# Spreading the second layer around the turn between two networks, and a new order for the last three pairs

## The chip, the cores and the metric

The kernel runs on one core of a Trainium2 chip. The metric is device time in microseconds (us) of one execution. Five engines matter: TensorE (PE, matrix products), VectorE (DVE), ScalarE (ACT), GpSimd (POOL), and the DMA queue that SyncE (SP) issues. PE writes to PSUM, eight banks of 512 single-precision columns by 128 partitions; VectorE and ScalarE read them and write there too, GpSimd does not.

## The reference

```python
# attention with a decay per head (4 batches, 8 heads, 576 positions, 64 wide), no softmax
ret = scale * (q @ k^T) * Dmat          # Dmat[i, j] = gamma_h ** (i - j) for i >= j, else 0
x = (ret @ v)                           # turned to 2304 tokens x 512
# mixture: 8 experts, 512 -> 1024 -> 512
P = exp(x @ w_gate - max); 8 rounds of normalising rows and columns of P
x = sum over e of P[:, e] * (relu(x @ w1[e]) @ w2[e])
# second network: 512 -> 2048 -> 512
h = x @ w_in
out = max(0.01 * h, h) @ w_out
```

## The kernel before, in words

After the attention, both networks run as one list of **units**. A unit is 512 hidden columns: the 8 experts give units 0 to 15 (`NU1` = 16, two per expert, `UPE`), the second network gives units 16 to 19. The 2304 tokens are held as two halves of 1152; one **step** takes a unit and a third of the tokens (`s` = 0, 1, 2; three tiles `jj` of 128 tokens from each half). So there are 60 steps, numbered 0 to 59 here: steps 42 to 44 are unit 14, steps 45 to 47 unit 15 (the last of the mixture), step 48 is the first of the second network. `edge` is 48, `NS` is 3.

Every product of two matrices is done with seven block products in place of eight (a Strassen form), and every operand is split into a high and a low half-precision part, so that one block product is several matmuls.

**First layer** (`product_h`, line 960): per step two groups `g` of 7 products, 14 in all (`PH`), each of six matmuls 384 wide, into the banks `hA`, `hB`, `hD`, `hE`. ScalarE and VectorE take them out, and `splits` (line 1021) makes from them the hidden tiles `hp` and `hs` (high part on ScalarE, low part on VectorE), the stationary operands of the second layer.

**Second layer** (`group_s`, line 1108): per step three **pairs** (one per `jj`; `pairs` counts them over all steps, 180), per pair five groups numbered `what` = 0 to 4, seven products of six matmuls 256 wide. A pair has two banks, `t1` (from `s1`, the tiles `s1a` and `s1b`) and `t2` (from `s2`, shown as `s`); pairs take the two bank pairs in turn (`at % 2`). Group 0: products 1 and 5 into the left and right half of `t1`; ScalarE copies the left half to the right half of `t2` (`seed`), and VectorE later adds the right half of `t1` to the result `yb` (`gather`, put off through the queue "evac" and issued at the latest before group 2). Group 1: product 6 onto the right half of `t2`, gathered to `ya`. Group 2: products 2 and 3 onto `t1`, gathered to `ya` 512 wide. Group 3: product 7 onto the right half of `t2`, copied to its left half. Group 4: product 4 onto the left half, and both halves gathered to `yb`. In units 0 and 15 (`PLAIN`) the second layer is done plainly, in four groups of six matmuls 512 wide (lines 1171 to 1190) and an empty group 4, from the hidden blocks as they are.

**The order.** All instructions are issued by one program in the order of the list `groups` (line 1332): group 0 of a pair stands before group 4 of the pair before it, so the list runs one group ahead; the last pairs of unit 15's steps are kept whole. `seconds_by(h)` (line 1349) tells how many groups are to be issued after `h` first-layer products: step `n`'s 15 groups (`GS`) begin at `14 (n + 1) + 6` (`LAG` = 6) and spread over `span` products. At the end of the program the rest of the list, the last 22 groups, runs with no first-layer products between. The other work (evacuations, weight preparation, the turn) stands in queues of `Order` (line 64), which books estimated times for each engine and issues a task when its inputs and its engine should be free; tasks that a product needs are forced out before it (`flush`, `need`). A queue looks at its first 12 tasks, the turn's at 48.

**The turn** (`turn_steps`, line 1247, and `operand_tasks`, line 467): when a pair of unit 15 is complete, its two result tiles are normed (sums on ScalarE or VectorE, factors on VectorE), scaled on GpSimd (line 1274), transposed on PE through an idle second-layer bank (line 1284), copied out, combined on GpSimd (lines 484 to 491), split on ScalarE and VectorE, stored to memory and loaded again as x of the second network. Steps 48, 49 and 50 need the x that steps 45, 46 and 47 end.

**Weights**: `prep_steps` (line 178) prepares unit `u + 1` while unit `u` runs: a load, eight magnitude sums (line 191), a maximum through PE, scaling on ScalarE, splits and differences on ScalarE and GpSimd. A second-layer weight buffer is free when the step two units back has ended.

Of the kernel before, what the change touches and what calls it, by code (L numbers as in the profile page):

```python
# [23 lines left out]
UPE = F // FU  # L24
# [7 lines left out]
NS = HT // ST  # L32
# [10 lines left out]
COST = {"A": (0.2, 0.00089), "D": (0.17, 0.00105), "G": (0.28, 0.0020)}  # L43
LAT, SLACK, WINDOW = 0.15, 0.6, (12, 48)
LAG = 6
PLAIN = (0, NU1 - 1)
XST, R64 = 4, 2

# [75 lines left out]
def retention_moe_ffn_kernel(ctx: ExitStack, tc: tile.TileContext, qk, vk, wg, wm, wf,  # L124
# [43 lines left out]
    order = Order()  # L168
# [9 lines left out]
    def prep_steps(u, small_bank):  # L178
# [105 lines left out]
        def add(eng, n, f, deps=(), key=None, cond=None, lat=LAT):  # L284
            x = Task(eng, n, f, deps, (u,) + key, cond, lat)
            tasks.append(x)
            return x
# [32 lines left out]
        def split(part, g, pre, key, cond=None):  # L320
            pre = tuple(pre)
            if part and u in PLAIN:
                hb = [add("A", 512, high_p(g, h), pre, key, cond) for h in range(2)]
# [206 lines left out]
    def bank_a(name):  # L530

        return ps.tile([P, 512], F32, tag="a", name=name, bufs=5)

    def bank_b(name):

        return ps.tile([P, 512], F32, tag="l1", name=name, bufs=1)
# [331 lines left out]
    hA, hB, hD, hE, s1a = (bank_a(n) for n in ("hA", "hB", "hD", "hE", "s1a"))  # L868
    s1 = [s1a, bank_b("s1b")]
    s2 = [ps.tile([P, 512], F32, tag=f"du{i}", name=f"s2_{i}", bufs=1) for i in range(2)]  # L870
# [72 lines left out]
    def work(tag, n=1, bufs=1):  # L943
        return gpool.tile([P, n, ST], F32, tag=tag, name=f"{tag}_{len(h_done)}", bufs=bufs)

    evac, until, h_last = {}, {}, {}
# [13 lines left out]
    def product_h(u, s, g, r):  # L960
# [50 lines left out]
        else:  # L1011
            order.flush("hid", lambda k: k[:3] != (u, s, g))
            tmp["fs"] = work("fs", 4)
            bent(tmp["fs"][:, 2] if u in PLAIN or u >= NU1 else D_, D_, u, HS)
            evac[4] = act()
# [5 lines left out]
    def splits(u, s, g, what):  # L1021
# [52 lines left out]
        else:  # L1074
            a11, a12, a22 = (fp[:, i] for i in range(3))
            d = evac[4]
            a21 = hD[:, :ST] if moe else fs[:, 2]
            if u in PLAIN:
                one = fs[:, 2:3]
# [28 lines left out]
    def group_s(u, s, jj, what):  # L1108

        j = NT_S * s + jj  # L1110
        ya, yb = y[j], y[NJ + j]
        if what == 0 and jj == 0:
            need_hid(u, s)
            if s == 0:
                need((u, "w2"))
            if u == UPE:
                order.flush("gate", lambda k: True)
            factors(u, s)
        fa, fb = fac[u][:, j:j + 1], fac[u][:, NJ + j:NJ + j + 1]
        at = pairs.index((u, s, jj))  # L1120
        t1, t2 = s1[at % 2], s2[at % 2]
        order.wait(until.get(("s", what < 2 if u in PLAIN else what in (0, 2), at % 2)))
        if what == 0:
            last_pair[0] = at
            if jj == 0:
                order.wait(h_last[u, s].done)
        left, right = slice(0, DH), slice(DH, DM)
        first = u == 0 or u == NU1
        ts = slice(128 * jj, 128 * jj + 128)

        def product(r, out_, start):
            xi, wi = PROD[r]
            k = 0
            for g in range(2):
                t, i = (hid[u, s, g, "p"], xi) if xi < 3 else (hid[u, s, g, "s"], xi - 3)
                w = wtiles[u, 1, g]
                for a, b in ((0, 0), (0, 1), (1, 0)):
                    nc.tensor.matmul(out_, t[:, a, i, ts], w[:, b, wi, 0, :], start=start and k == 0, stop=k == 5,  # L1138
                                     skip_group_check=True)
                    k += 1  # L1140
            order.t += 6 * (DH / 2400 + 0.004)

        def gather(out_, bank, f, new):
            n = bank.shape[-1]
            b = ("s", what < 2 if u in PLAIN else what in (0, 2), at % 2)
            ev = max(order.t + 0.2, until.get(b, 0.0) + LAT)
            if new:
                nc.scalar.activation(out_, bank, AF.Copy, scale=f)
                until[b] = order.book("A", n, ev)
            else:  # L1150
                nc.vector.scalar_tensor_tensor(out_, bank, f, out_, op0=ALU.mult, op1=ALU.add)  # L1151
                until[b] = order.book("D", n, ev)

        def seed(out_, bank):
            b = ("s", False, at % 2)
            nc.scalar.copy(out_, bank)  # L1156
            until[b] = order.book("A", DH, max(order.t + 0.2, until.get(b, 0.0) + LAT))
            if what == 0:
                until["s", True, at % 2] = until[b]

        def close():
            if jj == NT_S - 1:
                s_done.add((u, s))
            if u == NU1 - 1:
                turn_steps(s, j)

        if what == 0:
            if u == UPE:
                for i in (j, NJ + j):
                    nc.vector.tensor_scalar(y[i], y[i], prob[:, i, 0:1], None, op0=ALU.mult)  # L1170
        if u in PLAIN:
            if what == 4:
                return
            h, l = divmod(what, 2)
            bank = (t1, t2)[h].rearrange("p (a n) -> p a n", a=2)
            for g in range(2):
                part, i = (("p", l), ("p" if l else "s", 2 * l))[h]
                w, t = wtiles[u, 1, g][:, :, slice(1, 3) if l else slice(0, 4, 3), 0], hid[u, s, g, part]
                for q, (a, b) in enumerate(((0, 0), (0, 1), (1, 0))):
                    nc.tensor.matmul(bank, t[:, a, i, ts], w[:, b], start=l == g == q == 0, stop=l == g == 1 and q == 2,  # L1180
                                     skip_group_check=True)
                order.t += 3 * (DM / 2400 + 0.004)
                if g == 0:
                    tick(0)
            if l:
                gather((ya, yb)[h], (t1, t2)[h], (fa, fb)[h], first)
                if h:
                    close()
            tick(0)
            return  # L1190
        if what == 0:
            product(1, t1[:, left], True)
            tick(0)
            product(5, t1[:, right], False)
            seed(t2[:, right], t1[:, left])
            b = ("s", True, at % 2)
            sd = Task(None, 0, None, done=until[b])

            def f():
                gather(yb[:, right], t1[:, right], fb, first)  # L1200
            order.queues["evac"].append(Task("A" if first else "D", 0, f, (sd,), ("s", at)))
            tick(0)
        elif what == 1:
            product(6, t2[:, right], False)
            gather(ya[:, right], t2[:, right], fa, first)
            tick(0)
        elif what == 2:
            order.flush("evac", lambda k: k == ("s", at))
            order.wait(until.get(("s", True, at % 2)))
            product(2, t1[:, left], False)  # L1210
            tick(0)
            product(3, t1[:, right], False)
            if first:
                gather(ya[:, left], t1[:, left], fa, True)
                gather(ya[:, right], t1[:, right], fa, False)
            else:
                gather(ya, t1, fa, False)
            tick(0)
            if u == NU - 1:
                put(0, j)  # L1220
        elif what == 3:
            product(7, t2[:, right], False)
            seed(t2[:, left], t2[:, right])
            tick(0)
        else:
            product(4, t2[:, left], False)
            if first:
                gather(yb[:, left], t2[:, left], fb, True)
                gather(yb[:, right], t2[:, right], fb, False)
            else:  # L1230
                gather(yb, t2, fb, False)
            tick(0)
            if u == NU - 1:
                put(1, j)
            close()
# [69 lines left out]
    def tick(n):  # L1305

        order.t += n * (1 / 2400) + (0.009 if n else 0)
        wait[0] -= 1
        if drain and wait[0] <= 0:
            wait[0], f = drain.pop(0)  # L1310
            f()
        order.pump()
        try_loads()
# [17 lines left out]
    pairs = [(u, s, jj) for u, s in stages for jj in range(NT_S)]  # L1331
    groups = []
    whole = lambda p: p[0] == NU1 - 1 and p[2] == NT_S - 1
    for i, p in enumerate(pairs):
# [4 lines left out]
        if whole(p):  # L1339
            groups.append((*p, 4))  # L1340
    groups.append((*pairs[-1], 4))
    GS, PH = 5 * NT_S, 2 * len(H_ORDER)
    edge = stages.index((NU1, 0))
    spos, hpos = [0], [0]
# [4 lines left out]
    def seconds_by(h):  # L1349

        for n in range(len(stages) - 1, -1, -1):
            a = PH * (n + 1) + max(LAG, 13 - 3 * n)
            if h >= a:
                span = PH if n < edge - UPE * NS or n >= edge else PH - LAG
                return GS * n + min(GS, (h - a) * GS // span)
        return 0

# [101 lines left out]
```

## Time and profile before

| | |
|---|---|
| median of 3 runs | 1855.32 us (1853.75 to 1855.46) |
| profiled execution | 1855.54 us, span 1853.8 us, granted clock 0.988 |
| PE busy | 1795.8 us, 97% of the span, 13800 matmuls |
| VectorE, ScalarE, GpSimd busy | 1487.6 us (80%), 1261.7 us (68%), 823.9 us (44%) |
| chain that ended last | PE 87%, VectorE 6%, GpSimd 3%, ScalarE 1% |
| DMA | 276.67 MB, 48% of the 16 engines' time in the slices' mean |

How to read it: busy time of PE is the union of its matmuls, whose ends are modelled, so the distance between the starts of two products says more than the busy share. In the page's picture of 40 slices PE stands at 9 tenths almost everywhere; below it lie the first two slices, two from 1483 to 1576 us, where the second network begins, and the last. In a row of the timeline the bracket gives how long the engine was idle before, and which engine and line released it.

### The profile page before, as it was taken

Reading aid. Unit: us, or ns where it says so; the run is one execution under the profiler, and the core shown is the slowest. Engines: PE = TensorE matmul, PEld = TensorE weight load, DVE = VectorE, ACT = ScalarE, POOL = GpSimd, SP = SyncE. Lnnn points to the kernel's source line nnn. Section 1 sums busy time; section 2 is a strip of 40 time slices with the busy share of each in tenths; the row PEclk is TensorE's granted clock in tenths of the full one; section 3 lists DMA queues with packets and bytes.
Section 4 is the critical chain, followed back from the end, with each engine's and each line's share of the span. In section 5 each row is a group of like instructions: output and inputs, shape, how many; then the busy total and the mean of one; then the engine's idle time right before and its main releaser. Section 6 shows DMA issues by size and latency. Waiting matters only on the chain.

```text
span 1853.8 us, 35942 instructions
## 1 busy us (share of the span) xinstructions
PE 1795.8 (97%) x13800; PEld 1303.5 (70%) x13800; DVE 1487.6 (80%) x2576; ACT 1261.7 (68%) x2659; POOL 823.9 (44%) x786
## 2 busy tenths in 40 slices
PE   8899999999999999999999999999999987999997
PEld 7755577777777777777777777777675555777776
DVE  6755888998888888888888888888766885688875
ACT  5567677767676677767676777767565675876753
POOL 4633353626354453625254453726225961443600
PEclk9899999999999999999999999999999998999999
DMA  9874455355354454454354454455243454335242
GB/s 339 294 229 143 131 151 158 121 158 170 109 180 121 152 158 142 129 165 151 116 181 130 141 160 142 124 170 159 89 140 111 154 160 125 122 106 156 84 122 75
DMA packets 207857, 276.67 MB, mean 149 GB/s; under 512 B 13874, under 2 KB 177860, under 8 KB 202564
## 3 DMA queue, kind: packets, MB, share of 16 engines
q1 hardware_dynamic: 207684, 274.37, 47.4%
q8 instruction: 108, 1.77, 0.4%
q14 instruction: 65, 0.53, 0.1%
HBM read 244.69 MB, written 29.63 MB: 148 GB/s over the span
## 4 chain that ended last, share of the span: by engine, by line
PE 87%; DVE 6%; POOL 3%; ACT 1%; issue 1%; DMA 1%; SPq 0%; DVEq 0%; ACTq 0%; POOLq 0%
PE s L1138 16%; PE hB L968 12%; PE hA L968 12%; PE hE L968 12%; PE s1a L1138 11%; PE s1b L1138 11%; PE hD L968 6%; PE s L1180 2%; DVE y L1151 1%; PE s1a L1180 1%; PE sc L639 1%; PE s1b L1180 1%; PE xo L666 1%; DMA x<-x 1%; DVE xst L513 1%
## 5 line engine op out<-in xcount | busy, mean ns | idle before, releaser
L968 PEld LDWEIGHTS <-w 128*128 128x128 f16 x5040 | 492.0, 98 | 274.0 <-issue 14.0
L1138 PEld LDWEIGHTS <-hs 128*128 128x128 f16 x3888 | 380.3, 98 | 89.1 <-DVE hs L1059 5.8
L1138 PEld LDWEIGHTS <-hp 128*128 128x128 f16 x2916 | 285.7, 98 | 89.5 <-issue 12.9
L254 POOL TENSOR_TENSOR w<-raw,w 128x384 f16<-128x384 f32 x152 | 164.1, 1095 | 393.9 <-ACT w L244 393.8
L1151 DVE SCALAR_TENSOR_TENSOR y<-s,fac,y 128x256 f32<-128x256 f32 (+1 forms) x324 | 198.4, 614 | 114.7 <-PE s L1138 94.8
L261 POOL TENSOR_TENSOR raw<-raw 128x256 f32<-128x256 f32 x304 | 281.3, 925 | 20.0
L968 PE MATMUL hE<-x,w 128*128 128x384 f16 x1440 | 276.6, 327 | 6.1 <-DMA x<-x 2.9
L968 PE MATMUL hB<-x,w 128*128 128x384 f16 x1440 | 277.3, 328 | 4.4 <-ACT hB L978 4.3
L968 PE MATMUL hA<-x,w 128*128 128x384 f16 x1440 | 276.8, 328 | 4.2 <-ACT w L244 2.3
L1138 PE MATMUL s<-w,hs 128*128 128x256 f16 x1944 | 265.9, 273 | 1.6 <-ACT s L1156 1.5
L1059 DVE TENSOR_TENSOR hs<-fs,hs 128x768 f16<-128x768 f32 (+1 forms) x228 | 241.6, 1062 | 8.0 <-ACT hs L1049 7.1
L279 POOL TENSOR_TENSOR w<-raw,w 128x512 f16<-128x512 f32 x148 | 200.4, 1369 | 72.3 <-ACT w L273 71.8
L1049 ACT ACTIVATE hs<-fs 128x768 f16<-128x768 f32 (+1 forms) x228 | 187.6, 824 | 41.7 <-DVE fs L1084 32.0
L408 POOL TENSOR_TENSOR f<-f,e 128x256 f32<-128x256 f32 x64 | 54.9, 858 | 355.6 <-DVE e L400 355.6
L1049 ACT ACTIVATE hp<-fp 128x384 f16<-128x384 f32 x240 | 160.2, 677 | 11.8 <-DVE fp L1007 11.0
L1151 DVE SCALAR_TENSOR_TENSOR y<-s1a,fac,y 128x256 f32<-128x256 f32 (+1 forms) x161 | 98.6, 613 | 54.8 <-ACT s L1156 26.5
L1151 DVE SCALAR_TENSOR_TENSOR y<-s1b,fac,y 128x512 f32<-128x512 f32 (+1 forms) x163 | 99.9, 613 | 49.2 <-PE s1b L1138 22.6
L1138 PE MATMUL s1b<-w,hs 128*128 128x256 f16 x972 | 134.1, 274 | 5.1 <-DVE hs L1059 2.8
L1138 PE MATMUL s1a<-w,hp 128*128 128x256 f16 x972 | 133.2, 273 | 5.8 <-DVE mr L207 3.5
L968 PE MATMUL hD<-x,w 128*128 128x384 f16 x720 | 137.0, 326 | 0.0
L1138 PE MATMUL s1a<-w,hs 128*128 128x256 f16 x972 | 133.9, 273 | 2.8 <-ACT hs L1049 1.5
L1138 PE MATMUL s1b<-w,hp 128*128 128x256 f16 x972 | 133.3, 273 | 2.8 <-DVE y L1151 2.3
(199 smaller groups left out, 2694.7 us busy)
## 6 DMA issues: line engine op xcount, KB each, us to landing
x<-x SPq DMA_DIRECT2D x420, 384.0 KB, 4.1
raw<-in_wm SPq DMA_DIRECT2D x32, 1024.0 KB, 8.1
r<-in_wf SPq DMA_DIRECT2D x64, 256.0 KB, 2.7
qk<-in_qk SPq DMA_DIRECT2D x16, 512.0 KB, 5.8
vk<-in_vk SPq DMA_DIRECT2D x16, 512.0 KB, 5.8
wf_s<-f SPq DMA_DIRECT2D x32, 256.0 KB, 2.7
raw<-wf_s SPq DMA_DIRECT2D x8, 1024.0 KB
x<-xst SPq DMA_DIRECT2D x30, 256.0 KB, 2.8
```

Of the source, the lines that this page charges most:

```text
L254: nc.gpsimd.tensor_tensor(v[0], v[1], v[2], op=ALU.subtract)
L261: nc.gpsimd.tensor_tensor(o, x, y_, op=ALU.subtract)
L279: (nc.gpsimd if u or part else nc.vector).tensor_tensor(lo, r, hi, op=ALU.subtract)
L408: nc.gpsimd.tensor_tensor(dst, dst, cur["tx"].bitcast(F32), op=ALU.mult)
L513: nc.vector.tensor_tensor(st[d][:, :, 1], src[d](), st[d][:, :, 0], op=ALU.subtract)
L639: nc.tensor.matmul(scv[j][:w, m, :w], kv[r, m, :], qv[r, m, :], start=True, stop=True)
L968: nc.tensor.matmul(bank, w[:, a, wi, k, :], x[:, :, b, k, :], start=r in (1, 5) and k == q == 0, stop=k == 1 and q == 2, skip_group_check= ...
L1049: nc.scalar.activation(hid[k][:, 0, a:b], src[:, a:b], AF.Relu if moe and relu else AF.Copy)
L1059: nc.vector.tensor_tensor(t[:, 1, a:b], src[:, a:b], t[:, 0, a:b], op=ALU.subtract)
L1138: nc.tensor.matmul(out_, t[:, a, i, ts], w[:, b, wi, 0, :], start=start and k == 0, stop=k == 5, skip_group_check=True)
L1151: nc.vector.scalar_tensor_tensor(out_, bank, f, out_, op0=ALU.mult, op1=ALU.add)
L1180: nc.tensor.matmul(bank, t[:, a, i, ts], w[:, b], start=l == g == q == 0, stop=l == g == 1 and q == 2, skip_group_check=True)
```

## The change

Three things change. The squeeze of the second layer (`span`, line 1354) covered steps 42 to 47 with 8 products; now it covers steps 45 to 47 with 10, and steps 42 to 44 spread over 14 like all others. In step 59 the last pair (`at` = 179) takes `hA` and `hB` as its two banks, through the index `bi`, which also replaces `at % 2` in the keys of the booked times; its group 3 gathers the right half of `t2` at once, and its group 4 only the left half. And the last sixteen entries of `groups` are written out by hand: with A, B, C for the last three pairs and Z for the one before them, the order was A0 Z4 A1 A2 A3 B0 A4 B1 B2 B3 C0 B4 C1 C2 C3 C4 and is now A0 Z4 A1 B0 A2 B1 C0 A3 B2 C1 A4 B3 C2 C3 B4 C4. No product is added or removed; one gather is cut in two.

```diff
--- before.py
+++ after.py
@@ -43,6 +43,7 @@
 COST = {"A": (0.2, 0.00089), "D": (0.17, 0.00105), "G": (0.28, 0.0020)}
 LAT, SLACK, WINDOW = 0.15, 0.6, (12, 48)
 LAG = 6
+EARLY = 4
 PLAIN = (0, NU1 - 1)
 XST, R64 = 4, 2
 
@@ -1118,8 +1119,9 @@
             factors(u, s)
         fa, fb = fac[u][:, j:j + 1], fac[u][:, NJ + j:NJ + j + 1]
         at = pairs.index((u, s, jj))
-        t1, t2 = s1[at % 2], s2[at % 2]
-        order.wait(until.get(("s", what < 2 if u in PLAIN else what in (0, 2), at % 2)))
+        bi = 2 if at == len(pairs) - 1 else at % 2
+        t1, t2 = (*s1, hA)[bi], (*s2, hB)[bi]
+        order.wait(until.get(("s", what < 2 if u in PLAIN else what in (0, 2), bi)))
         if what == 0:
             last_pair[0] = at
             if jj == 0:
@@ -1142,7 +1144,7 @@
 
         def gather(out_, bank, f, new):
             n = bank.shape[-1]
-            b = ("s", what < 2 if u in PLAIN else what in (0, 2), at % 2)
+            b = ("s", what < 2 if u in PLAIN else what in (0, 2), bi)
             ev = max(order.t + 0.2, until.get(b, 0.0) + LAT)
             if new:
                 nc.scalar.activation(out_, bank, AF.Copy, scale=f)
@@ -1152,11 +1154,11 @@
                 until[b] = order.book("D", n, ev)
 
         def seed(out_, bank):
-            b = ("s", False, at % 2)
+            b = ("s", False, bi)
             nc.scalar.copy(out_, bank)
             until[b] = order.book("A", DH, max(order.t + 0.2, until.get(b, 0.0) + LAT))
             if what == 0:
-                until["s", True, at % 2] = until[b]
+                until["s", True, bi] = until[b]
 
         def close():
             if jj == NT_S - 1:
@@ -1193,7 +1195,7 @@
             tick(0)
             product(5, t1[:, right], False)
             seed(t2[:, right], t1[:, left])
-            b = ("s", True, at % 2)
+            b = ("s", True, bi)
             sd = Task(None, 0, None, done=until[b])
 
             def f():
@@ -1206,7 +1208,7 @@
             tick(0)
         elif what == 2:
             order.flush("evac", lambda k: k == ("s", at))
-            order.wait(until.get(("s", True, at % 2)))
+            order.wait(until.get(("s", True, bi)))
             product(2, t1[:, left], False)
             tick(0)
             product(3, t1[:, right], False)
@@ -1221,12 +1223,15 @@
         elif what == 3:
             product(7, t2[:, right], False)
             seed(t2[:, left], t2[:, right])
+            if bi == 2:
+                gather(yb[:, right], t2[:, right], fb, False)
             tick(0)
         else:
             product(4, t2[:, left], False)
-            if first:
-                gather(yb[:, left], t2[:, left], fb, True)
-                gather(yb[:, right], t2[:, right], fb, False)
+            if first or bi == 2:
+                gather(yb[:, left], t2[:, left], fb, first)
+                if first:
+                    gather(yb[:, right], t2[:, right], fb, False)
             else:
                 gather(yb, t2, fb, False)
             tick(0)
@@ -1339,6 +1344,9 @@
         if whole(p):
             groups.append((*p, 4))
     groups.append((*pairs[-1], 4))
+    end = [(p, w) for p, w in zip((0, -1, 0, 1, 0, 1, 2, 0, 1, 2, 0, 1, 2, 2, 1, 2),
+                                  (0, 4, 1, 0, 2, 1, 0, 3, 2, 1, 4, 3, 2, 3, 4, 4))]
+    groups[-16:] = [(*pairs[p - 3], w) for p, w in end]
     GS, PH = 5 * NT_S, 2 * len(H_ORDER)
     edge = stages.index((NU1, 0))
     spos, hpos = [0], [0]
@@ -1351,7 +1359,7 @@
         for n in range(len(stages) - 1, -1, -1):
             a = PH * (n + 1) + max(LAG, 13 - 3 * n)
             if h >= a:
-                span = PH if n < edge - UPE * NS or n >= edge else PH - LAG
+                span = PH - EARLY * (edge - NS <= n < edge)
                 return GS * n + min(GS, (h - a) * GS // span)
         return 0
 
```

## Rows read from the trace of the kernel before

**Rows 1.** Windows: stretch; its length; busy time (instructions) by engine; granted clock; DMA share; GB/s

```profile
160.00:1300.00 1140.00, 1136.09 (x8532) 832.36 (x8530) 980.69 (x1720) 813.47 (x1702) 530.68 (x509) 1.00 0.48 147
1330.00:1340.00 10.00, 7.51 (x48) 4.72 (x46) 7.44 (x11) 5.21 (x9) 2.98 (x2) 0.86 0.28 79
```

**Rows 2.** Timeline of PE, end of step 43: start, length, instructions, idle before

```profile
1333.68 0.49 PE L1138 MATMUL s1b<-w,hs 128*128 128x256 f16 x3
1336.06 0.39 PE L1138 MATMUL s1b<-w,hs 128*128 128x256 f16 x2 [1.89 <-ACT hs L1049]
...
1337.17 2.08 PE L968 MATMUL hA<-x,w 128*128 128x384 f16 x6
1339.05 1.91 PE L968 MATMUL hE<-x,w 128*128 128x384 f16 x6
1340.80 1.14 PE L968 MATMUL hB<-x,w 128*128 128x384 f16 x6
```

**Rows 3.** Timeline of PE, end of step 44

```profile
1365.60 0.49 PE L1138 MATMUL s1a<-w,hs 128*128 128x256 f16 x3
1367.30 0.39 PE L1138 MATMUL s1a<-w,hs 128*128 128x256 f16 x2 [1.21 <-ACT hs L1049]
1368.29 0.28 PE L1138 MATMUL s1a<-w,hs 128*128 128x256 f16 x1 [0.60 <-DVE hs L1059]
```

**Rows 4.** Timeline of PE, start of step 50

```profile
1524.41 0.82 PE L1138 MATMUL s1b<-w,hs 128*128 128x256 f16 x6
1526.71 1.14 PE L968 MATMUL hA<-x,w 128*128 128x384 f16 x6 [1.48 <-DMA x<-x]
1527.68 0.82 PE L1138 MATMUL s<-w,hs 128*128 128x256 f16 x6
1531.41 1.79 PE L968 MATMUL hE<-x,w 128*128 128x384 f16 x6 [2.91 <-DMA x<-x]
...
1535.38 1.14 PE L968 MATMUL hB<-x,w 128*128 128x384 f16 x6
```

**Rows 5.** Timeline of PE, start of step 51

```profile
1561.88 0.82 PE L1138 MATMUL s1a<-w,hs 128*128 128x256 f16 x6
1564.98 0.50 PE L968 MATMUL hA<-x,w 128*128 128x384 f16 x2 [2.28 <-ACT w L244]
...
1575.89 1.27 PE L968 MATMUL hB<-x,w 128*128 128x384 f16 x6
```

**Rows 6.** Timeline of ScalarE: magnitude sums of unit 17's weights

```profile
1523.36 0.62 ACT L191 ACTIVATE junk<-raw 128x512 bf16<-128x512 f32 x1
...
1545.35 0.61 ACT L191 ACTIVATE junk<-raw 128x512 bf16<-128x512 f32 x1
```

**Rows 7.** Line 1274 on GpSimd: least, median, longest in ns; first and last start

```profile
L1274 POOL TENSOR_SCALAR y<-y,ts x18: 1559/1644/2779, 1412.7 to 1506.8; 128x512 f32<-128x512 f32 x18
```

**Rows 8.** Timeline of PE, the last pair

```profile
1843.67 0.82 PE L1138 MATMUL s<-w,hs 128*128 128x256 f16 x6
1845.51 0.81 PE L1138 MATMUL s1b<-w,hp 128*128 128x256 f16 x6 [1.02 <-DVE y L1151]
...
1846.82 0.82 PE L1138 MATMUL s<-w,hs 128*128 128x256 f16 x6
1848.08 0.81 PE L1138 MATMUL s<-w,hp 128*128 128x256 f16 x6 [0.44 <-ACT s L1156]
```

**Rows 9.** Timeline of VectorE, the last pair's gathers

```profile
1843.93 1.14 DVE L1151 SCALAR_TENSOR_TENSOR y<-s,fac,y 128x512 f32<-128x512 f32 x2 [1.92 <-PE s L1138]
1844.98 0.48 DVE L1151 SCALAR_TENSOR_TENSOR y<-s1b,fac,y 128x256 f32<-128x256 f32 x1
...
1848.99 0.75 DVE L1151 SCALAR_TENSOR_TENSOR y<-s,fac,y 128x512 f32<-128x512 f32 x1 [1.22 <-PE s L1138]
```

**Rows 10.** Timeline of VectorE, reading a bank behind ScalarE

```profile
1359.11 0.56 DVE L1002 SCALAR_TENSOR_TENSOR fp<-hB,p 128x384 f32<-128x384 f32 x1 [0.51 <-ACT hD L996]
```

**Rows 11.** DMA issues of the last stores: count, KB each, median us to landing

```profile
out<-y SPq DMA_DIRECT2D x4, 128.0 KB, 2.4
```

## The prediction

> **What bounds the kernel now.** I read the windows first, to see where TensorE (PE) is not full. From 160 to 1300 us it is busy 1136.09 of 1140 us at full clock [rows 1]: there nothing but its own work counts. A change of order can only win in the rest, so I followed PE's timeline there. What it loses is the excess of start-to-start distances over the undisturbed ones, 0.97 us for a first-layer product (six matmuls) and 0.66 us for a second-layer one, both read off where such rows come. Five places matter.
>
> At the end of step 43 the first group of the next step is issued right behind the last first-layer product, and its last three matmuls wait for hidden tiles that ScalarE and VectorE are still splitting. Three matmuls take 0.33 us, so 1333.68 to 1336.06 loses 2.05 us and 1336.06 to 1337.17 another 0.78. The next two first-layer products then run 1.88 and 1.75 us apart in place of 0.97 (0.9 and 0.8 lost) [rows 2]: the granted clock, 1.0 elsewhere, is 0.86 in the mean of 1330 to 1340 [rows 1], so for a while it stood at the lower level, 1.2 GHz, after those waits. Together 4.5 us.
>
> One step later the same happens: 1.70 - 0.33 = 1.37 and 0.99 - 0.22 = 0.77 us [rows 3], 2.1 us. Here the short waits are followed by no slow products.
>
> At the start of step 50 PE waits for the turned x. From 1524.41 to 1526.71 it loses 2.30 - 0.66 = 1.6; 1526.71 to 1527.68 is an undisturbed first-layer product; from 1527.68 to 1531.41 it loses 3.1; and the three products to 1535.38 take 3.97 in place of 0.97 + 2 x 0.66, 1.7 more [rows 4].
>
> At the start of step 51 the weights of unit 17 are late. From 1561.88 to 1575.89 four second-layer and two first-layer products run, 4 x 0.66 + 2 x 0.97 = 4.6 us of work in 14.0: 9.4 us lost [rows 5].
>
> In the last sixteen groups PE stops three times between a pair's groups 1 and 2 (1843.67 to 1845.51 is 1.84 - 0.66 = 1.18; the other two are 1.13 and 1.19) and once before the last group (1.26 - 0.66 = 0.60); 1845.51 to 1846.82 shows two undisturbed products. Together 4.1 us [rows 8].
>
> **First part: steps 42 to 44 are no longer squeezed.** A step's 15 groups go between first-layer products, from the 6th product of the next step on. Before, steps 42 to 47 did it within 8 products, so they ended exactly with that next step, and where units run in plain order of the list the last of the 15 is already the first group of the step after it. Its hidden tiles come from the product just issued: this is what rows 2 and 3 show. Spread over 14 products this group comes six products later, as in the steps of [rows 1], which lose next to nothing. The split chain takes 3.5 us (1333.68 to 1337.17), six products alone 5.8, so it is covered. No instruction is added or removed; 7 of the 15 groups move past first-layer products. Gain 4.5 + 2.1 = 6.6 us. Bounds: 4.9 if the clock loss of 1.7 comes elsewhere instead, and 6.6, all that the rows hold; I take 6.6, by the like steps of rows 1. At the boundary after step 44 PE doesn't wait now, so nothing is won there. What could be late next is whatever needs the end of these steps: the second-layer weight buffers of unit 16 wait for step 44, now 6 products later. But the weight queue looks only 12 tasks ahead, and the twelve before them wait for the first half of step 47 in any case, which hides it; uncovered it is those six products, 5.8 us, off a preparation that has the whole of step 48 left.
>
> **Second part: steps 45 to 47 spread over 10 products, not 8.** Their y is turned (scaled, transposed, summed, split, stored, loaded) into the x of steps 48 to 50. A step's three tiles are complete 1, 1 and 2 first-layer products later than before. PE waits for a load of x only at step 50 [rows 4], so steps 48 and 49 have cover. At step 50 the last tile's transposes wait for the buffers of the tile before it; it is that tile's delay, one product, that passes on: +1.0 us. Bounds: 0 (the looser spread lets VectorE and ScalarE, which serve turn and groups together, be faster by as much) and 1.95 (two products). Shorter waits for scaled y inside steps 48 and 49 I leave as they are. Behind step 50 all moves along, unit 17's weights included, so the 9.4 us stay; the rivals hold their bounds.
>
> **Third part: the last three pairs over three bank pairs.** The products stay 22. A pair's group 2 overwrites its first bank, so it waits for the gather of that bank's right half, which stands on VectorE behind two others (start to start 1.05 us for these two, then 0.48 for itself [rows 9]). In the new order two groups or more lie between a pair's 1 and 2. I followed all sixteen with 0.66 us per product, 0.66 and 0.39 from a wide and a narrow gather to the next, and 0.44 from a product past ScalarE's copy to the next product (end of 1846.82's to 1848.08 [rows 8]): each of the three gathers ends 0.2 to 2.8 us before its bank is wanted, in whichever of the two places VectorE's order gives it. So 1.13, 1.18 and 1.19 go, and the 0.60 too, since that copy now lies beside the second pair's last group. New is a wait: the last pair's right half is gathered behind that copy, on the same bank. Two engines that only read one bank are ordered in this kernel: VectorE stood 0.51 us for ScalarE's copy out of hB before it read hB itself [rows 10]. So the gather ends 0.49 us after PE could have begun the last group; only the final gather is queued behind it. That is 256 wide instead of 512, 0.75 - 0.48 = 0.27 less [rows 9]. Sum 4.1 - 0.49 + 0.27 = 3.9 us. Of the banks taken, hA and hB, the last first-layer readers are done before these groups begin. Issue, landing and end of the last stores I take as they are, 2.4 us to landing [rows 11]. Bounds: 1.5 (the last three gathers end within 2.2 us of each other, so gathers queue and stores crowd) and 4.4 (no order between readers).
> The Trainium skill, "DMA: Bandwidth & Descriptors", section "Latency and other measured facts", puts most of a transfer's fixed cost on the receipt from HBM, 0.2 us on average and 2 us at high load. By that rule the crowded last stores could land up to 1.8 us later, an estimate from that page, and this part would be worth 2.1. The trace has no crowded stores that bear it out.
>
> **Sum.** -6.6 + 1.0 - 3.9 = -9.5 us on the profiled execution of 1855.54 us (span 1853.8). The median of the runs is 0.2 lower than it. Forecast **1846.0**, with 1842 to 1850 as its own range.
>
> **Rivals.**
> *The turn slows (1854).* POOL scales 18 tiles in 1.56 to 2.78 us each, median 1.64 [rows 7]; the six of the last step stand in the chain to step 50's x. If the new spread puts VectorE's splits beside them so that all take the longest, that is 6 x 1.14 = 6.8 us, and 0.95 for the second product: 1846.0 + 7.8 = 1853.8. For it: both engines are crowded there. Against: the same work stands in nearly the same order, and the longest is rare. The Trainium skill, "SBUF — State Buffer", section "Who interferes with whom", has the mechanism: a VectorE operation with two SBUF inputs and a reading GpSimd instruction exclude each other. By that rule the spread from 1.56 to 2.78 is what one would see; no row names the partner.
>
> *Unit 17's weights fall behind (1863, slower).* The last of the eight magnitude sums comes at 1545.35, 22 us after the one before [rows 6], because ScalarE is booked for other work; what follows it is forced at the start of step 51. If the later turn pushes that sum to the forced point, 1562.5, the chain behind it moves by 17.2 us: 1846.0 + 17.2 = 1863. It beats the whole gain from a slip of 9.5 us on. For it: the choice goes by booked times and has jumped 22 us already. Against: the turn moves by a product or two.
>
> *They come in time (1837).* If that sum goes out beside its neighbours, up to 9.4 us of step 51 go: 1846.0 - 9.4 = 1836.6. For and against as above, mirrored.
>
> *The third part doesn't do what it says* (a gather elsewhere in VectorE's order than I followed): 3.9 less, 1849.9, inside the forecast's own range.
>
> **Chances.** Forecast 0.50, slow turn 0.18, late weights 0.14, early weights 0.18. About 0.2%, 3.7 us, is what a measurement of this kernel can tell from no change. The slow turn (1850 to 1855) splits half between faster and same, and a few per cent of forecast and late weights are same. Faster 0.76, same 0.10, slower 0.14. The range goes from 1838.5 (the best third of the early weights cut) to 1855 (the late weights outside).
>
> **What would show it.** The second layer's waits for hidden tiles at the ends of steps 43 and 44 are gone, and the dip of the granted clock with the first. Step 50's wait for x is about a product longer. The last sixteen groups run their 22 products with the one wait for a hidden tile in front and one of half a microsecond before the last group. I am wrong if the boundary waits stay or return two products later, or if the loss at step 50 or 51 changes by more than 3 us.

## The result and the profile after

The kernel after takes 1834.0 us in the median of 4 runs (1829.28 to 1836.26), the kernel before 1854.53 in the median of 4 (1851.93 to 1855.46): a ratio of 0.9888, 95% interval [0.9864, 0.9912]. The forecast was 1846.0, and 1834.0 lies below its range. The profiled execution of after took 1832.41 us, span 1830.6, granted clock 0.993; its span is 23.1 us shorter than that of before (1830.63 and 1853.76 in the two traces).

To see where these 23.1 us went I read PE's timeline of each kernel at six marks. First-layer products are counted through the program: step n begins with number 14n + 1, product 651 is the seventh of step 46, product 700 the last of step 49, 714 the last of step 50. Between two marks both kernels have the same products to do. Starts in us:

| mark | before | after | stretch up to it: before | after | difference |
|---|---|---|---|---|---|
| step 42 | 1271.37 | 1266.90 | 1271.37 | 1266.90 | -4.47 |
| product 651 | 1402.70 | 1391.56 | 131.33 | 124.66 | -6.67 |
| step 50's second product | 1531.41 | 1520.73 | 128.71 | 129.17 | +0.46 |
| step 51's third product | 1575.89 | 1556.81 | 44.48 | 36.08 | -8.40 |
| step 52 | 1600.85 | 1581.64 | 24.96 | 24.83 | -0.13 |
| end of the span | 1853.76 | 1830.63 | 252.91 | 248.99 | -3.92 |

The first line is not the change: up to step 42 both kernels run the same instructions. The next five are, 18.7 us in sum.

A window of after at the end of step 43 (length; busy time and instructions of PE, weight loads, VectorE, ScalarE, GpSimd; granted clock; DMA share; GB/s):

```profile
1319.00:1329.00 10.00, 10.00 (x79) 7.51 (x77) 8.43 (x13) 6.60 (x15) 7.06 (x7) 1.00 0.48 141
```

PE's timeline of after at the ends of steps 43 and 44 (start, length, instruction, idle before):

```profile
1322.66 0.82 PE L1140 MATMUL s1b<-w,hs 128*128 128x256 f16 x6
1323.32 1.14 PE L969 MATMUL hA<-x,w 128*128 128x384 f16 x6
1324.29 0.82 PE L1140 MATMUL s<-w,hs 128*128 128x256 f16 x6
...
1350.07 0.82 PE L1140 MATMUL s1a<-w,hs 128*128 128x256 f16 x6
1350.72 1.14 PE L969 MATMUL hA<-x,w 128*128 128x384 f16 x6
```

The four waits that PE had at these two places in before (three stand in [rows 2, 3], the fourth is 0.60 us at 1337.06) are gone, the next product follows a group after 0.66 us, and the granted clock is 1.00 in place of 0.86 [rows 1]. The same timeline at the starts of steps 50 and 51:

```profile
1515.16 0.82 PE L1140 MATMUL s1b<-w,hs 128*128 128x256 f16 x6
1516.14 1.14 PE L969 MATMUL hA<-x,w 128*128 128x384 f16 x6 [0.16 <-DMA x<-x]
1517.12 0.82 PE L1140 MATMUL s<-w,hs 128*128 128x256 f16 x6
1520.73 2.10 PE L969 MATMUL hE<-x,w 128*128 128x384 f16 x6 [2.80 <-DMA x<-x]
...
1549.81 0.82 PE L1140 MATMUL s1a<-w,hs 128*128 128x256 f16 x6
1550.47 1.14 PE L969 MATMUL hA<-x,w 128*128 128x384 f16 x6
1551.44 0.82 PE L1140 MATMUL s<-w,hs 128*128 128x256 f16 x6
1552.41 0.50 PE L969 MATMUL hE<-x,w 128*128 128x384 f16 x2
1553.90 0.66 PE L969 MATMUL hE<-x,w 128*128 128x384 f16 x3 [0.99 <-POOL w L280]
...
1556.81 1.14 PE L969 MATMUL hB<-x,w 128*128 128x384 f16 x6
```

At step 50 the waits for x are 0.16 and 2.80, where they were 1.48 and 2.91 [rows 4]. At step 51 the six products of [rows 5] take 1549.81 to 1556.81, 7.0 us in place of 14.0; the 2.28 us wait for ScalarE's first split is gone. What is left above the 4.6 us of work is for the most part two waits for GpSimd's last splits (line 280), 0.99 and 0.76 us. The preparation of unit 17 in ScalarE's timeline says why. It is a chain: eight magnitude sums, four over the first-layer and four over the second-layer weights; their maximum and from it the scale; four scalings of the first-layer weights; and the splits of their first half, which step 51's first product needs. First and last of the four late magnitude sums, first and last scaling, first split:

```profile
1508.46 0.63 ACT L192 ACTIVATE junk<-raw 128x512 bf16<-128x512 f32 x1
...
1512.83 0.63 ACT L192 ACTIVATE junk<-raw 128x512 bf16<-128x512 f32 x1
...
1531.86 0.71 ACT L230 ACTIVATE raw<-raw,sw 128x512 f32<-128x512 f32 x1
...
1539.30 0.71 ACT L230 ACTIVATE raw<-raw,sw 128x512 f32<-128x512 f32 x1
...
1540.29 0.50 ACT L245 CAST w<-raw 128x384 f16<-128x384 f32 x1
```

The same three last rows in before:

```profile
1551.37 0.71 ACT L229 ACTIVATE raw<-raw,sw 128x512 f32<-128x512 f32 x1
...
1563.80 0.72 ACT L229 ACTIVATE raw<-raw,sw 128x512 f32<-128x512 f32 x1
1564.42 0.92 ACT L244 CAST w<-raw 128x384 f16<-128x384 f32 x2
```

All four sums now lie within 4.4 us, where the last two were 22 us apart [rows 6], and the first split begins 10.2 us before step 51 (1550.47 - 1540.29), not 0.6 us before it (1564.98 - 1564.42). The last sixteen groups, on PE and then on VectorE, and the last stores:

```profile
1824.15 0.82 PE L1140 MATMUL s<-w,hp 128*128 128x256 f16 x6
1825.28 0.82 PE L1140 MATMUL hB<-w,hp 128*128 128x256 f16 x6 [0.31 <-DVE y L1153]
```

```profile
1825.14 0.74 DVE L1153 SCALAR_TENSOR_TENSOR y<-s,fac,y 128x512 f32<-128x512 f32 x1
1826.13 0.48 DVE L1153 SCALAR_TENSOR_TENSOR y<-hB,fac,y 128x256 f32<-128x256 f32 x1 [0.25 <-PE hB L1140]
```

```profile
out<-y SPq DMA_DIRECT2D x4, 128.0 KB, 2.3
```

The stops of [rows 8] are gone. One new wait is there, before the last group: 1824.15 to 1825.28 is 1.13 - 0.66 = 0.47 us. The final gather is the narrow one, 0.48 in place of 0.75 [rows 9], and the last stores land in 2.3 us, before in 2.4 [rows 11].

### The profile page after: what moved, and what is told of

It reads as the page before. It is cut to its first block, busy times and chain, and to the rows that moved or that the text cites. A ratio compares the mean times of both kernels' runs of the same rounds, so it can differ in the third digit from the quotient of the medians.

```text
span 1830.6 us, 35943 instructions
## 1 busy us (share of the span) xinstructions
PE 1784.7 (97%) x13800; PEld 1298.3 (71%) x13800; DVE 1485.3 (81%) x2578; ACT 1259.0 (69%) x2658; POOL 821.4 (45%) x786
## 4 chain that ended last, share of the span: by engine, by line
PE 86%; DVE 5%; DMA 4%; POOL 2%; ACT 1%; issue 1%; SPq 0%; ACTq 0%; DVEq 0%; POOLq 0%
PE s L1140 17%; PE hB L969 12%; PE hA L969 12%; PE hE L969 12%; PE s1a L1140 11%; PE s1b L1140 11%; PE hD L969 6%; PE s L1182 2%; DMA vk<-in_vk 1%; PE s1a L1182 1%; DMA x<-xst 1%; PE s1b L1182 1%; DVE y L1153 1%; DMA x<-x 1%; DMA gq<-in_c_gq 1%
## 5 line engine op out<-in xcount | busy, mean ns | idle before, releaser
L1153 DVE SCALAR_TENSOR_TENSOR y<-s1b,fac,y 128x256 f32<-128x256 f32 (+1 forms) x161 | 98.6, 613 | 47.0 <-ACT s L1158 19.4
L1140 PE MATMUL s<-w,hp 128*128 128x256 f16 x966 | 131.8, 273 | 0.0
```

## The experiments

The parts one by one came first; then what moves unit 17's weights. Of each edit only the lines that matter are shown here. In the table, stretch a goes from product 651 to step 50's second product, b from there to step 51's third, and "split" says how the first eight splits and sums of the first half of unit 17's first-layer weights are issued, one by one behind products 706 to 712, or all in a block behind 714, where step 51 demands them (this column is read from the order of the instructions in the program, the rest from PE's timelines). The last four splits of this half go out behind 713 or 714 in every run. The expectations of e9 and e10 speak of a second half; by the program it is the first (`("w1", 0)`).

| run | 42 to 651 | a | b | split |
|---|---|---|---|---|
| before | 131.33 | 128.71 | 44.48 | block |
| after | 124.66 | 129.17 | 36.08 | one by one |
| e1 | 124.66 | 127.93 | 44.42 | block |
| e2 | 131.34 | 129.98 | 34.88 | one by one |
| e3 | 129.66 | 128.52 | 44.50 | block |
| e4 | 129.66 | 133.52 | 38.54 | one by one |
| e5 | 129.65 | 129.20 | 42.96 | block |
| e6 | 124.65 | 130.93 | 42.05 | block |
| e7 | 124.66 | 142.22 | 44.18 | block |
| e8 | 124.66 | 133.00 | 31.04 | one by one |
| e9 | 129.65 | 128.51 | 37.48 | one by one |
| e10 | 124.66 | 128.62 | 41.88 | block |
| e11 | 124.65 | 128.03 | 40.40 | one by one |

The column b holds more than the start of step 51. From the start of the last group before step 51's first product to its third product, 14.0 us in [rows 5], all runs with the block take 13.0 to 14.0 us, and those one by one 7.0 (e11 8.4, e8 5.0).

**e1: the first part alone** (on before: 42 to 44 as wide as all, 45 to 47 squeezed to 8).

```diff
-span = PH if n < edge - UPE * NS or n >= edge else PH - LAG
+span = PH - LAG if edge - NS <= n < edge else PH
```

> The first part alone: steps 42 to 44 spread over 14 products, steps 45 to 47 stay at 8, old order at the end. Theory: the 8.4 us won at step 51 come from the second part (with 10 products the turn is issued sooner and leaves ScalarE free for the last magnitude sum of unit 17), so here that sum is issued behind the 706th first-layer product as before, and only the two boundary waits go: -6.6 us, ratio 0.9964, the loss at the start of step 51 still 8 to 10 us. Rival (the relaxed steps 42 to 44 are what frees ScalarE at step 50): -15 us, ratio 0.992, and a loss at step 51 of 1 to 2 us.

Measured: 0.9963 [0.9948, 0.9979]. The boundary waits are gone, and b stays at 44.42.

**e2: the second part alone** (on before: 42 to 44 squeezed to 8, 45 to 47 to 10).

```diff
+span = PH - (4 if n >= edge - NS else LAG) * (edge - UPE * NS <= n < edge)
```

> The second part alone: steps 42 to 44 stay at 8 products, steps 45 to 47 at 10, old order at the end. Theory: the last magnitude sum comes behind the 698th product, the weights of unit 17 are in time, -8 us (ratio 0.9957), while the boundary waits at the ends of steps 43 and 44 stay. Rival (the first part did it): no change or +1 us from the later turn, ratio 1.000 to 1.0005.

Measured: 0.9963 [0.9951, 0.9975]. The boundary waits are there, and b falls by 9.6 us. So it is the second part, which I had forecast to cost 1.0, that brings the weights in time. ScalarE's timeline, last scaling and first split; step 51 begins at 1559.44:

```profile
1548.27 0.71 ACT L229 ACTIVATE raw<-raw,sw 128x512 f32<-128x512 f32 x1
1549.26 0.50 ACT L244 CAST w<-raw 128x384 f16<-128x384 f32 x1
```

**e3: the third part alone** (on before: bank pairs and order of the last sixteen groups, as in the change).

> The third part alone, the order of the last three pairs. Both theories: -3.9 us, ratio 0.9979; nothing else moves. In the profile the last sixteen groups have one wait of about 1 us on a hidden tile and one of about 0.5 us before the last group.

Measured: 0.9976 [0.9963, 0.9988], some 4.4 us of 1852.62. The three parts alone give 6.9 + 6.9 + 4.4 = 18.2 us of run time, each by its interval good to 2 or 3 us. The change gives 20.8 of run time (16.3 to 25.2 by its interval) and 18.7 of span behind step 42. Within that noise they add up.

**e4: the four magnitude sums issued at once**, as soon as the weights are there (on before; a task with `now` set skips the demand that the planner must book its engine as free).

```diff
+            for x in xs_:
+                x.now = u == NU1 + 1 and part == 1
```

> The kernel before, with one rule changed: the four magnitude sums of the second-layer half of unit 17's weights are issued as soon as their data should be there, without the demand that ScalarE be booked free within 0.6 us; they then come behind the 693rd first-layer product instead of the 693rd, 696th, 699th and 706th. Theory (the late last sum is what makes unit 17's weights late): the loss at the start of step 51 falls from 9.4 us to 0 to 3, -6 to -9 us, ratio 0.9955 to 0.9968. Rival (GpSimd, still full of the turn, or ScalarE behind the sums decides): the loss stays above 7 us, ratio 0.999 to 1.001.

Measured: 0.9994 [0.9983, 1.0006]. b fell by 5.9 us, and a rose by 4.8. The four sums stand on ScalarE in one go, 2.9 us (1507.36 to 1510.25), ahead of the copy that PE's next group needs. PE's timeline:

```profile
1505.15 1.14 PE L971 MATMUL hA<-x,w 128*128 128x384 f16 x6
1510.66 1.44 PE L1141 MATMUL s<-w,hs 128*128 128x256 f16 x6 [4.38 <-ACT s L1159]
```

and ScalarE's, with the first and the last sum and the copy:

```profile
1507.36 0.63 ACT L191 ACTIVATE junk<-raw 128x512 bf16<-128x512 f32 x1
...
1509.62 0.63 ACT L191 ACTIVATE junk<-raw 128x512 bf16<-128x512 f32 x1
...
1510.25 0.36 ACT L1159 COPY s<-s1a 128x256 f32<-128x256 f32 x1
```

The gain is real and is spent ahead of time, some 50 us before step 51.

**e5: only the last two sums tied to product 699** (on before).

```diff
+                for x in xs_[2:]:
+                    x.cond, x.now = lambda: there() and hpos[0] >= 699, True
```

> The kernel before, with only the last two of unit 17's eight magnitude sums tied to the 699th first-layer product (where the third of the four stands anyway; the last moves there from the 706th). Theory (the late last sum makes the weights late, and four sums in one go cost ScalarE's next copy in the run before this one): the loss at the start of step 51 falls to 1 to 3 us with nothing lost at step 49, -7 to -8.5 us, ratio 0.9955 to 0.9963. Rival (what the second part won came from the turn's load on GpSimd and VectorE, not from the sum's place): the loss stays above 7 us, ratio 0.999 to 1.001.

Measured: 1.0000 [0.9991, 1.0010]. My theory, that the late last sum is what makes the weights late, fell here. ScalarE's timeline, last scaling and first split:

```profile
1549.56 0.71 ACT L229 ACTIVATE raw<-raw,sw 128x512 f32<-128x512 f32 x1
...
1559.71 0.92 ACT L244 CAST w<-raw 128x384 f16<-128x384 f32 x2
```

The scaled weights are there 9.4 us before the first split, and nobody splits them: the split is not issued until step 51 demands it.

**e6: the last sum held to product 706** (on after).

```diff
+            late = lambda: there() and hpos[0] >= 706
```

> The changed kernel, with the last of unit 17's magnitude sums held back to the 706th first-layer product, its place in the kernel before. Theory: the loss at the start of step 51 comes back, 8 to 9 us more than the changed kernel, ratio to the kernel before 0.9925 to 0.9945. Rival (as above): as the changed kernel, 0.988 to 0.990.

Measured: 0.9952 [0.9935, 0.9968], a little more loss than the theory's 0.9925 to 0.9945: b is back at 42.05. The loss can be brought back by the sum, but e5 shows that the sum's place is not enough.

**e7: a squeeze of two in place of four** (on after).

```diff
-EARLY = 4
+EARLY = 2
```

> The changed kernel with EARLY = 2: steps 45 to 47 spread over 12 products. The sums of unit 17 then end behind the 697th product. Theory: step 51 keeps its gain; y of each step is complete one or two products later still, so the wait for x at step 50 grows by 1 to 2 us if the turn is what sets it, and not at all if the turn's own chain sets it. Ratio to the kernel before 0.988 to 0.9895.

Measured: 1.0034 [1.0023, 1.0045], slower than before, which I had not expected. The x of step 50 is late, which is what the prediction's rival of the slow turn would show. PE's timeline:

```profile
1524.30 2.08 PE L969 MATMUL hA<-x,w 128*128 128x384 f16 x6 [4.66 <-DMA x<-x]
1533.51 2.10 PE L969 MATMUL hE<-x,w 128*128 128x384 f16 x6 [5.84 <-DMA x<-x]
```

Product 651 starts at 1391.29, in after at 1391.56, but the turn's last transposes come at 1513.8 against 1504.9. The rival's mechanism, slower scalings on GpSimd, isn't there: line 1279 in e7, then in after (least, median, longest in ns; first and last start),

```profile
L1279 POOL TENSOR_SCALAR y<-y,ts x18: 1561/1756/2574, 1402.3 to 1510.6; 128x512 f32<-128x512 f32 x18
L1279 POOL TENSOR_SCALAR y<-y,ts x18: 1562/1776/2532, 1402.1 to 1497.5; 128x512 f32<-128x512 f32 x18
```

takes about as long in both, and its last instruction starts 13.1 us later. So these scalings come later; they aren't slower. Why by 13 us, when y is complete a product or two later, stays open. And the splits stand in the block again, so b is 44.18: the gain is gone and a is 13 us longer than after's.

**e8: step 48 squeezed to ten as well** (on after).

```diff
-span = PH - EARLY * (edge - NS <= n < edge)
+span = PH - EARLY * (edge - NS <= n <= edge)
```

> The changed kernel with step 48 squeezed to 10 products as well, so that four more groups stand ahead of the second product of step 50, which waits for x. Theory (x comes when it comes, PE only lacks other work): the wait of 2.8 us and the slow products behind it go, -3 to -4.5 us against the changed kernel, ratio to the kernel before 0.986 to 0.987. Rival (x comes later by as much, since VectorE's turn work stands behind more gathers, or step 49's hidden tiles are waited for): 0.988 to 0.990.

Measured: 0.9891 [0.9873, 0.9909], in the rival's range, and the interval overlaps that of after. This run's a and b can't be set beside the others': six second-layer products, 6 x 0.66 = 4.0 us, stand ahead of the mark between them here and behind it there. The sum of a and b is 164.0 us, after's 165.3. The wait for x at step 50's second product is gone, but PE then waits for hidden tiles, in part 1.91 us:

```profile
1531.99 0.39 PE L1140 MATMUL s1b<-w,hs 128*128 128x256 f16 x2 [1.91 <-ACT hs L1050]
```

What separated 44 from 36 in b was by then the column "split". Its gate, in the order of issue, is the scale, worked out ahead of the scalings, mostly on VectorE: issued behind 704 or earlier in all runs that split one by one, and behind 706 or 707 in all with the block. Two runs test that.

**e9: only this chain let through** (on before; e5's edit, and the total, the maximum and the scale of unit 17's weights also with `now`).

```diff
+            for x in ts_:
+                x.now = key == ("w1", 0) and x.key[0] == NU1 + 1
```

> The kernel before, with two demands dropped for the second half of unit 17's first-layer weights alone: its last two magnitude sums go out behind product 699, and its total, top and scale as soon as what they read is there, without waiting until the model has VectorE free. By the issue order this puts the scale behind product 704 (before: 707), the last prescale behind 706 (before: 714) and the two high splits, two low splits and four sums behind 708 to 711 instead of all behind 714, the last product before step 51. Turn, squeeze and tail are those of before. Theory (what counts is that these eight steps no longer stand in one block at 714): from step 50's second product to step 51's third 35 to 39 us instead of 44.5, ratio 0.9945 to 0.9970. Rival (the gain of the change comes from the shorter turn or from the load on ScalarE, and pieces moved forward only push back others, as with the four sums at 693): the same stretch is given back between products 699 and 715, ratio 0.9985 to 1.0010.

Measured: 0.9968 [0.9957, 0.9980]; b 37.48, and nothing given back in a (128.51). Behind step 52 it gives back 1.0 us (253.94 to the end of the span, in before 252.91). Up to step 52 the kernel wins 7.3 us against before (651 to 52: 190.82 and 198.15), the second part alone 8.5 (189.69). ScalarE's timeline, last scaling and first split:

```profile
1543.62 0.71 ACT L229 ACTIVATE raw<-raw,sw 128x512 f32<-128x512 f32 x1
...
1546.86 0.50 ACT L244 CAST w<-raw 128x384 f16<-128x384 f32 x1
```

**e10: only this scale held back, to product 706** (on after).

```diff
+            hold = (lambda: hpos[0] >= 706) if (u, *key) == (NU1 + 1, "w1", 0) else None
```

> The kernel after, with one instruction held: the scale of unit 17's second half isn't issued before product 706 (after: 704). By the issue order the prescales move from 705..708 to 706..709 and the eight splits and sums from 709..712 into the block behind 714; the magnitude sums stay at 696 to 698. Theory: the two products' delay of one instruction is enough to bring the loss back; from step 50's second product to step 51's third 41 to 45 us instead of 36, ratio 0.9920 to 0.9950. Rival (the place of the magnitude sums, or the turn, is what counts): stretch 35 to 38 us, ratio 0.9870 to 0.9905.

Measured: 0.9938 [0.9925, 0.9952]; b 41.88. The sums stay together (1512.27 to 1516.65). ScalarE's timeline from the first scaling, and PE's at step 51:

```profile
1539.65 0.72 ACT L230 ACTIVATE raw<-raw,sw 128x512 f32<-128x512 f32 x1 [0.69 <-DVE sw L219]
...
1544.25 0.71 ACT L230 ACTIVATE raw<-raw,sw 128x512 f32<-128x512 f32 x1
...
1554.40 0.92 ACT L245 CAST w<-raw 128x384 f16<-128x384 f32 x2
```

```profile
1554.97 0.50 PE L970 MATMUL hA<-x,w 128*128 128x384 f16 x2 [1.67 <-ACT w L245]
```

As in e5 the weights lie scaled for 9.4 us (1544.96 to 1554.40) and PE then waits for their split. One step of the chain, issued two products later, brings back 5.8 of the 8.4 us. By the order of issue, ScalarE's next places, behind products 710 to 712, go to step 50's hidden tiles and a copy of a second-layer group; splits that miss the places behind 709 find none until step 51 demands them. In e5 it is the same.

**e11: the squeeze of six with this chain** (the edits of e9 on after with `EARLY = 6`).

> The kernel after with the squeeze of steps 45 to 47 put back to six (so the second layer of unit 15 and the turn are where they stand in the kernel before), and with the two demands of e9 dropped, so that unit 17's second half is split behind 708 to 711. Theory (four instead of six matters only through those splits): ratio 0.9870 to 0.9915, no worse than the kernel after by more than 0.002. Rival (the squeeze of four has a worth of its own, in the turn or in step 48): 0.9925 to 0.9960.

Measured: 0.9922 [0.9908, 0.9935], between the ranges of theory and rival. Order and waits at step 51 are those of e9, but b is 2.9 us longer, with the granted clock low in windows where e9's stood at 1.00 (1537 to 1547 and 1558 to 1570):

```profile
1538.00:1543.00 5.00, 4.27 (x20) 2.45 (x21) 3.62 (x7) 3.78 (x8) 0.00 (x0) 0.71 0.00 0
1562.00:1568.00 6.00, 6.00 (x39) 4.13 (x38) 1.98 (x3) 3.96 (x9) 4.18 (x5) 0.84 0.00 0
```

That profile also reached step 42 3.6 us later than after's. So this run doesn't settle whether four instead of six has a worth beyond the splits; the medians leave 5 us (1839.02 and 1834.0) open.

## Why the prediction was wrong, step by step

- *First part, -6.6.* Right: -6.67 in the profile and 0.9963 alone. But 1.7 of it is the clock, and that is not fixed, so the close match is in part luck: of the six kernels with the old squeeze in steps 42 to 44, before and e2 took 131.3 us from step 42 to product 651, e3, e4, e5 and e9 129.7. The lower bound, 4.9, was the better figure for what the edit itself gives (129.65 - 124.66 = 5.0).
- *Second part at step 50, +1.0.* Measured +0.46 up to there with the first part in it; the second part alone gives +1.27 (e2), the first alone -0.78 (e1), so the size was right; what gives the -0.78 stays open. e7 shows that x can be much later. GpSimd's scaling took 1562, 1776 and 2532 ns at the least, in the median and at the longest, where it took 1559, 1644 and 2779 [rows 7], so the slow-turn rival didn't come with a squeeze of four. By the Trainium skill's "SBUF — State Buffer", section "Who interferes with whom", a VectorE instruction with two SBUF inputs contends with a GpSimd instruction that reads SBUF; the spread is still there, and no row names the partner.
- *"Behind step 50 all moves along, unit 17's weights included, so the 9.4 us stay."* This is the step that failed. The program decides its order by booked times, so the late weights were no fixed loss that moves along: at the start of step 51 the loss fell by 7.0 us, and b by 8.4. The second part changed which of ScalarE's tasks were issued first: by the order of issue, the turn's last copies go out behind products 693 and 694 (before: 695 and 696) though y is complete two products later, and the sums follow at 696 to 698 (before: 693, 696, 699, 706), the scale at 704 (before: 707), the splits at 709 to 712 (before: 714). Shown on the chip: the second part does it (e2), moving this chain alone in before wins 7.3 us up to step 52 (e9), and holding its scale for two products costs 5.8 (e10). That the turn's earlier end is what freed ScalarE for the sums is read from the order of issue alone; no run isolates it.
- *The rival "they come in time"* had the outcome, at 1837, and only half the mechanism. It rested on the last sum alone, and on the reading that all behind that sum is forced at step 51. In before the scale goes out behind 707 and three scalings behind 708 and 709, unforced; only the last scaling and the splits stand behind 714. e5 put the sum beside its neighbours and gained nothing. What counts is that the splits are issued before step 51 forces them.
- *Third part, -3.9.* Right: -3.92, the new wait 0.47 against 0.49, the final gather 0.27 shorter. The Trainium skill's "DMA: Bandwidth & Descriptors", section "Latency and other measured facts", puts access to HBM at 0.2 us on average and 2 us at high load; by an estimate from that page crowded last stores could have cost up to 1.8 us more. The trace shows 2.3 us to landing against 2.4, so none of that.
- *The rest.* The terms that were forecast right make -6.67 + 0.46 - 3.92 = -10.1, stretch b -8.40, step 52 another -0.13: 18.7. Of b, 7.0 is the start of step 51; the other 1.4 lies ahead of it, where among others before's wait of 0.81 us for the weights' maximum is gone. The other 4.5 us of the two profiles lie before step 42, where both run the same instructions, and are no effect of the change.

## What to carry to other kernels

Where a program places work by booked times, a loss further down is not a constant that moves along: an edit upstream redraws the order, and the term to work out is when the late chain is issued, not only when its engine is free. Look for work that lies ready while nobody has issued it (in e5 and e10, 9.4 us between the last scaling and the first split): the place to act is the rule that issues it, not the operations ahead of it. And a cure that puts four operations in one go on a shared engine (e4) can give the gain back at the next consumer.

## What was unexpected of the hardware

The same waits need not be followed by the same clock. After 1.89 + 0.60 us of waiting at the end of step 43 the clock fell in before [rows 1, 2]; after the same two waits it did not fall in e2 or e3, but in e2 it fell one step later, after 1.21 + 0.60, where before shows nothing [rows 3]. Up to these places e2 and e3 run the same instructions as before. Windows of e2 around the two ends, and PE's rows after the second:

```profile
1328.00:1338.00 10.00, 7.51 (x58) 5.21 (x56) 7.65 (x12) 5.67 (x10) 3.11 (x3) 1.00 0.28 79
1363.00:1373.00 10.00, 8.56 (x43) 4.67 (x44) 3.35 (x6) 6.68 (x16) 0.00 (x0) 0.83 0.35 138
```

```profile
1364.95 2.02 PE L968 MATMUL hA<-x,w 128*128 128x384 f16 x6
1366.76 1.98 PE L968 MATMUL hE<-x,w 128*128 128x384 f16 x6
1368.58 1.14 PE L968 MATMUL hB<-x,w 128*128 128x384 f16 x6
```

Two products stand 1.8 us before the next one in place of 0.97; for a while the clock stood at its lower level, 1.2 GHz. That is 1.7 us that one profile has and another lacks, at the same place of the same instructions. What decides it no run here shows.

And the start varies. The same instructions brought the 13 profiles to step 42 between 1266.63 and 1271.37 us. Of the 4.47 us between before and after, 4.31 are there at the first product of step 0 (102.91 and 98.60 us). The granted clock in the windows from 40 to 80 us differs, first before, then after:

```profile
40.00:80.00 40.00, 36.57 (x447) 32.38 (x447) 31.24 (x53) 24.57 (x60) 23.22 (x25) 0.79 0.85 294
```

```profile
40.00:80.00 40.00, 34.90 (x498) 31.06 (x499) 31.20 (x57) 26.85 (x66) 26.16 (x29) 0.91 0.93 336
```

The clock isn't all of it: e7 and e8 both had 0.96 there and reached step 42 at 1266.63 and 1269.23. So a difference of two spans is to be cut into stretches, and those with the same instructions put aside, before it is explained.
